# Gated linear attention and a rational MLP on one core: a sixth plain pair of feature blocks, the turned k in another bank, a new order

## The chip, the core and the metric

One core of a Trainium2 chip runs one program. TensorE (PE) multiplies matrices, VectorE (DVE), ScalarE (ACT) and GpSimd (POOL) work on elements, SyncE (SP) issues most DMAs. Each engine works through its own queue in order and waits on semaphores for the others. Time is device microseconds of an execution, the median of the runs shown.

## The reference

3072 tokens (4 batches of 768), 8 heads of 48. Per head a state decays by alpha and takes in an outer product of k and v; its product with q is the attention's output, 384 values for each token. These go through an MLP of 2048 features whose activation is a quotient of polynomials.

```
for t in range(S):
    state = alpha[:, :, t, :, None] * state + einsum('bhd,bhe->bhde', k[:, :, t], v[:, :, t])
    y[:, :, t] = einsum('bhd,bhde->bhe', q[:, :, t], state)
h = x @ w_in
P = a[0] + a[1]*h + a[2]*h*h + a[3]*h*h*h
Q = 1.0 + abs(b[0])*abs(h) + abs(b[1])*h*h
out = (P / (Q + 1e-06)) @ w_out
```

## The kernel before

**Attention** goes in 24 groups g of 128 tokens. DVE turns alpha, q and k into place (`turn_a`, `turn_qk`; the first four groups are turned by PE instead, L439, and copied by ACT, L458), scans alpha from both ends (`suffix` L476, `prefix` L488), and the results scale k and q (L497, L500). PE turns k (`k_turn`, L551), ACT copies it out (`k_evac`, L554); PE makes the scores (`sc_mm`, L518) and the values' outer products (`kv_mm`, L582). The scores are copied out in two halves, each on ACT (L539) or DVE (L541), and masked by POOL (L545); DVE adds up the state (L610, L613), and ACT or POOL places it beside the values (L568). Then PE does the attention product (`attn_mm`, L600), and ACT copies it into x (L630, L634), its rest being taken by DVE (L638).

**The MLP** is a list of jobs u. A plain job takes 256 tokens and a pair of feature blocks (2 x 128 features) through FP32 matmuls (`plain_in` L680, `plain_out` L693). A wide job takes 512 tokens and one block, with x, the weights and the result each split into a high part and a rest, and three products for one (`wide_in` L707, `wide_out` L726; the last 512 tokens use L720 and L735). The plain jobs cover the first JP = 5 pairs of the first 512 tokens, 10 jobs; wide jobs do the rest, 6 blocks of the first 512 tokens and all 16 blocks of the other five supers m of 512. Between in and out of a job stand ACT's absolute value (L762), linear term (L765) and reciprocal (L793), POOL's or ACT's parts of Q (L769, L771, L774) and five steps of DVE (L785, L789, L803, L806, L812); the last of these, called g, frees the bank of the job's input product, which is used again three jobs later (`bank(u % 3)`). Wide jobs then split the result (L815 on ACT, L819 on POOL or DVE).

**Weights** come as pairs of 32-bit words of doubles and are put together by five steps for each key (a pair of blocks of w_in, "i", or w_out, "o"): `join_scale` (L285, ACT or POOL), `join_low` (L293, DVE), `join_sign` (L297 on ACT, L299 on DVE) and `join` (L313, DVE). Keys under JP are kept whole for the plain jobs, in place; later an SP load (`bring`, L321) brings each back to be split for the wide jobs (`split_hi` L328, `split_lo`). Other keys are split at once.

**A guard** loads alpha in 18 pieces and checks its bounds, two activations of ACT for each (L865); the sums (L875, L878, L881) decide at the end whether the fast result stands.

**Banks.** ps is the accumulator memory of eight banks. Scores go to banks 4 and 5 (SCB and SCB + 1), the values' products to columns from 256 of both, the attention product to bank 4, the turned k to bank 4. A column of bank 5 (`floor_q`) holds the floor that the scans read from the fifth group on.

**The order.** Every step is declared by `add` with its engine, its steps to wait for and its engines to choose from. ORDER, a packed table of numbers, sets the sequence of all steps and which of the engines does a step that has a choice; each engine executes its steps in that order. A step waits for the steps listed with it:

```
was = [("xh", g - 1), ("xl", g - 1), ("km", g - 1), ("kv", g - 1), ("se", g - 1, 0), ("se", g - 1, 1)]
add(("kt", g), "PE", 0.38, k_turn, (g,), [("k", g)] + was + near, lat=0.13)
add(("s", g), "PE", SV[0], sc_mm, (g,), [("k", g), ("q", g), ("ke", g)] + was + near, lat=0.13)
```

Here kt is the k turn, ke its copy, s the scores, vk the values' products, se the two score copies, xh and xl the readers of the attention product, km and kv the two state sums. The builder adds waits wherever a step touches memory that another engine uses, by banks for ps.

Of the kernel before, what the change touches and what calls it, by code (L numbers as in the profile page):

```python
# [74 lines left out]


ORDER = [
    'c-jq?gO(*a5CGGi?sSs1ZQHhO+qS)XcV>35wr$(CZQHi--Zxa8Qx!=~R!X6YsiG-Sq*yr>Lm3rCMOS0hI5l3)SBunQ6;-WN',
# [4 lines left out]
    '6q=54C_Y`$DJi)sqME9rs+h`5S?H>siL<boN<cSNLaMK_tKzDvT7-*(Qc)sGO;ITt&Bi&n1k+G9%1Sw@wQ8&8;sRWTX(=6@',
    'S7+5VwG;=ahw72a9<mVU;e5<N8*x+6ZDmz@%0(HdiK?b<sr%}+%1wEwASI?GREP@Ga?D8Aba|>knW!igqwD&HUV(SiTa}lJ',
    'P;q*v+Nm}wAJwILRDznTfO@VvsVb_v3Q}FvAoW8%RXtU2wGu1QDjcXPQdKHRrRa%zrCzGL>V;Z^>v1hs4yi)xuo~s30#u(G',
    'P-$uyvH=^>8}&hzq3TqF?y1$d8Mg%0q{dW>now8OS#?wGRWH>?^;Lt_5Y?K>QX6VYZK)acQ~d)S)Hb}S+fxVXNxi5y4OQi+',
    '9c{$}*fDSpo6{}*UVT)3sUIE0?y5(iHf_f`)Q5K9SM^hUQwn~oFY2HAt^geTQemnEwWI)bBn_RYGX<;RYB+sXpVThwPk+@P',
# [50 lines left out]
    '(y#K>eGOmJFZ0WNX<y4X_bq%&-^#c4wS67m#<%q~T|3|2ckms3C*Rq3@m+m4-`)4{J$)a)!mswdd~d(juk-7Dec#vr2X6hG',
    'js',
# [1085 lines left out]
```

## Time and profile before

| | |
|---|---|
| median of 3 runs | 522.44 us (521.91 to 522.75) |
| profiled execution, its own time | 521.38 us |
| its span | 519.3 us |
| PE busy | 499.3 us, 96% |
| DVE busy | 473.2 us, 91% |
| ACT busy | 411.0 us, 79% |
| POOL busy | 404.8 us, 78% |

Busy time is that of the whole span. The terms below come from the profiled execution, which lies 1.06 us under the median.

### The profile page before, as it was taken

Reading aid. Unit: us, or ns where it says so; the run is one execution under the profiler, and the core shown is the slowest. Engines: PE = TensorE matmul, PEld = TensorE weight load, DVE = VectorE, ACT = ScalarE, POOL = GpSimd, SP = SyncE. Lnnn points to the kernel's source line nnn. Section 1 sums busy time; section 2 is a strip of 40 time slices with the busy share of each in tenths; the row PEclk is TensorE's granted clock in tenths of the full one; section 3 lists DMA queues with packets and bytes.
Section 4 is the critical chain, followed back from the end, with each engine's and each line's share of the span. In section 5 each row is a group of like instructions: output and inputs, shape, how many; then the busy total and the mean of one; then the engine's idle time right before and its main releaser. Section 6 shows DMA issues by size and latency. Waiting matters only on the chain.

```text
span 519.3 us, 13513 instructions
## 1 busy us (share of the span) xinstructions
PE 499.3 (96%) x5094; PEld 412.3 (79%) x5094; DVE 473.2 (91%) x729; ACT 411.0 (79%) x756; POOL 404.8 (78%) x419
## 2 busy tenths in 40 slices
PE   8877899999999999999999999999999999999995
PEld 7776778788887788878888788888888787789895
DVE  3997999999999999999999999999989899898793
ACT  3879999999899877868777777886878778776564
POOL 3253765989999999788989988797896779667673
PEclk9997999999999999999999999999999999999999
DMA  9989945554555545653456454344625400050001
GB/s 246 307 240 245 279 104 130 146 119 110 119 127 136 123 92 130 106 112 84 86 120 124 93 133 84 90 86 102 143 50 116 82 1 1 3 101 1 0 1 64
DMA packets 146708, 57.56 MB, mean 111 GB/s; under 512 B 133456, under 2 KB 139216, under 8 KB 146640
## 3 DMA queue, kind: packets, MB, share of 16 engines
q1 hardware_dynamic: 146496, 56.57, 46.6%
q8 instruction: 41, 0.67, 0.5%
q14 instruction: 27, 0.22, 0.1%
q10 hardware_dynamic: 144, 0.10, 0.1%
HBM read 47.98 MB, written 4.72 MB: 101 GB/s over the span
## 4 chain that ended last, share of the span: by engine, by line
PE 63%; ACT 11%; DVE 6%; POOL 6%; DMA 5%; SPq 5%; issue 4%; POOLq 0%; DVEq 0%; ACTq 0%
PE ps L707 26%; PE ps L726 22%; PE ps L600 3%; PE ps L693 3%; SPq L415 2%; PE ps L720 2%; DMA wi_words<-in_moe_w_in_dram 2%; POOL gh_gl L819 2%; ACT wo_words L297 2%; PE ps L518 2%; PE ps L582 2%; PE ps L680 2%; POOL qm L774 1%; ACT ps L793 1%; DVE t L789 1%
## 5 line engine op out<-in xcount | busy, mean ns | idle before, releaser
L707 PE MATMUL ps<-x,wi 128*128 128x512 f32 x774 | 197.7, 396 | 0.7 <-DVE t L812 0.6
L707 PEld LDWEIGHTS ps<-x,wi 128*128 128x128 f32 x774 | 142.6, 188 | 32.6 <-DVE t L812 2.6
L726 PE MATMUL ps<-gh_gl,wo 128*128 128x512 f32 x630 | 162.5, 396 | 0.1
L774 POOL TENSOR_TENSOR qm<-qm,ah 128x512 f32<-128x512 f32 x96 | 124.1, 1294 | 23.4 <-ACT qm L771 20.3
L726 PEld LDWEIGHTS ps<-gh_gl,wo 128*128 128x128 f32 x630 | 115.8, 188 | 25.6 <-POOL gh_gl L819 0.9
L819 POOL TENSOR_TENSOR gh_gl<-t,gh_gl 128x512 fp32r<-128x512 f32 x83 | 107.4, 1297 | 21.0 <-ACT gh_gl L815 12.6
L793 ACT ACTIVATE ps<-qm 128x512 f32<-128x512 f32 x96 | 57.7, 602 | 36.6 <-DVE t L789 17.7
L803 DVE SCALAR_TENSOR_TENSOR t<-t,coef,ps 128x512 f32<-128x512 f32 x96 | 70.8, 737 | 12.7 <-ACT ps L793 11.3
L765 ACT ACTIVATE t<-ps,coef 128x512 f32<-128x512 f32 x96 | 65.4, 684 | 14.2 <-POOL gh_gl L819 9.5
L789 DVE SCALAR_TENSOR_TENSOR t<-t,coef,ps 128x512 f32<-128x512 f32 x96 | 70.7, 738 | 1.5
L785 DVE TENSOR_TENSOR t<-t,ps 128x512 f32<-128x512 f32 x96 | 64.9, 677 | 6.8 <-ACT t L765 5.2
L812 DVE SCALAR_TENSOR_TENSOR t<-ps,t 128x512 f32<-128x512 f32 x96 | 65.6, 684 | 1.5
L806 DVE SCALAR_TENSOR_TENSOR ps<-qm,ps 128x512 f32<-128x512 f32 x96 | 65.8, 685 | 0.0
L762 ACT ACTIVATE ah<-ps 128x512 f32<-128x512 f32 x96 | 56.4, 590 | 9.6 <-PE ps L707 8.3
L815 ACT ACTIVATE gh_gl<-t 128x512 fp32r<-128x512 f32 x86 | 53.6, 625 | 6.6 <-DVE t L812 5.9
L769 POOL TENSOR_SCALAR qm<-ah,bab 128x512 f32<-128x512 f32 x42 | 32.4, 772 | 18.9 <-ACT ah L762 7.1
L545 POOL TENSOR_SCALAR_AFFINE_SELECT tqk<-tqk 64x512 f32<-64x512 f32 x48 | 31.4, 655 | 18.7 <-ACT tqk L539 8.2
L771 ACT ACTIVATE qm<-ah,bab 128x512 f32<-128x512 f32 x54 | 38.9, 721 | 0.5
L476 DVE TENSOR_TENSOR_SCAN tg<-ta,ps 128x528 f32<-128x528 f32 x24 | 29.7, 1241 | 8.6 <-ACT ta L458 7.3
L720 PE MATMUL ps<-wo,gh_gl 128*128 128x384 f32 x180 | 33.7, 336 | 0.0
L497 POOL TENSOR_TENSOR tqk<-tqk,tg 128x512 f32<-128x512 f32 x22 | 28.4, 1289 | 6.5 <-ACT tqk L458 6.3
L720 PEld LDWEIGHTS ps<-wo,gh_gl 128*128 128x128 f32 x180 | 31.8, 188 | 1.2
(112 smaller groups left out, 701.5 us busy)
## 6 DMA issues: line engine op xcount, KB each, us to landing
raw_a<-in_alpha_dram SPq DMA_DIRECT2D x160, 48.0 KB, 2.2
wi_words<-in_moe_w_in_dram SPq DMA_DIRECT2D x8, 768.0 KB, 6.5
wo_words<-in_moe_w_out_dram SPq DMA_DIRECT2D x8, 768.0 KB, 6.4
sv<-in_v_dram SPq DMA_DIRECT2D x48, 96.0 KB, 2.6
wr<-in_alpha_dram SPq DMA_DIRECT2D x18, 256.0 KB, 3.1
raw_qk<-in_k_dram SPq DMA_DIRECT2D x80, 48.0 KB, 2.3
raw_odd<-in_k_dram SPq DMA_DIRECT2D x80, 48.0 KB, 2.1
raw_qk<-in_q_dram SPq DMA_DIRECT2D x80, 48.0 KB, 2.3
```

Source lines behind the costliest of these rows:

```text
L707: nc.tensor.matmul(h_of(u), w(key)[:, kt * FU + f % FU, :], x[:, kt, xp, :], start=(n == 0), stop=(n == len(todo) - 1),)
L720: nc.tensor.matmul(bank(T_BANKS[tt], DM), g[:, tt * P : (tt + 1) * P], w(("o", f // FU))[:, f % FU, :], start=(f == 0 and first_w), stop=( ...
L726: nc.tensor.matmul(bank(O_BANKS[dt]), w(("o", f // FU))[:, f % FU, dt * P : (dt + 1) * P], g, start=(f == 0 and first_w), stop=(f == NF - ...
L765: nc.scalar.activation(buf(s, "t1", u), h_of(u), AF.Identity, bias=a2, scale=a3_reg)
L774: nc.gpsimd.tensor_tensor(buf(s, "qm", u), buf(s, "qm", u), buf(s, "ah", u), op=ALU.mult)
L785: nc.vector.tensor_tensor(t, t, h_of(u), op=ALU.mult)
L789: nc.vector.scalar_tensor_tensor(t, t, a1, h_of(u), op0=ALU.add, op1=ALU.mult)
L793: nc.scalar.add_instruction(mybir.InstActivation(name=nc.get_next_instruction_name(), engine=nc.scalar.engine, func=AF.Reciprocal, ins=[nc ...
L803: nc.vector.scalar_tensor_tensor(t, t, a0, h_of(u), op0=ALU.add, op1=ALU.mult)
L806: nc.vector.scalar_tensor_tensor(h_of(u), buf(s, "qm", u), Q_ONE, h_of(u), op0=ALU.add, op1=ALU.mult)
L812: nc.vector.scalar_tensor_tensor(t, h_of(u), 2.0, t, op0=ALU.subtract, op1=ALU.mult, reverse0=True)
L819: eng.tensor_tensor(buf(s, "gl", u).rearrange("p a b -> p (a b)"), buf(s, "t1", u), gh, op=ALU.subtract)
```

## The change

JP goes from 5 to 6: the first 512 tokens have 12 plain jobs and 4 wide ones, where it was 10 and 6. Jobs are 96 either way. Keys 5 of w_in and w_out are now kept whole and brought back later by two SP loads. The k turn and its copy use bank 5; the turn waits for kv and se of the group before it, no longer for xh, xl and km. The scores still wait for all six. ORDER is a new table (2733 steps where there were 2737), which also chooses engines anew: of the score copies ACT does 45 of 48 where it did 43, of the signs 13 of 16 where it did 12, of the rests of results POOL does 82 where it did 83. In a new program all lines behind the table are one less.

```diff
 ORDER = [
-    'c-jq?gO(*a5CGGi?sSs1ZQHhO+qS)XcV>35wr$(CZQHi--Zxa8Qx!=~R!X6YsiG-Sq*yr>Lm3rCMOS0hI5l3)SBunQ6;-WN',
...
+    'c-jq@gO(ji5CErpx_c1Ywr$(CZQIGs?q(6&wr$(CZQFS7AL>+{im8-BHC{ziPDNL-lvj~d6ct&KimE0kR-$64iE5!*qNb{8',
...
-JP = 5
+JP = 6
...
     def k_turn(g):
         for a in range(NPAIR):
-            nc.tensor.transpose(bank(SCB)[:, a * KW : (a + 1) * KW], tk[g % NQ][0:KW, a, :], ident[0:KW, 0:KW])
+            nc.tensor.transpose(bank(SCB + 1)[:, a * KW : (a + 1) * KW], tk[g % NQ][0:KW, a, :], ident[0:KW, 0:KW])
 
     def k_evac(g):
-        nc.scalar.activation(kts[g % NSC][:, 0 : NC4 * KW], bank(SCB, NC4 * KW), AF.Copy)
+        nc.scalar.activation(kts[g % NSC][:, 0 : NC4 * KW], bank(SCB + 1, NC4 * KW), AF.Copy)
...
-        add(("kt", g), "PE", 0.38, k_turn, (g,), [("k", g)] + was + near, lat=0.13)
+        add(("kt", g), "PE", 0.38, k_turn, (g,), [("k", g)] + was[3:] + near, lat=0.13)
```

In the rows of the order, t_100 to t_102 are the results in work of three jobs in turn, tqk_88 to tqk_90 the turned q and k of three groups in turn, ps the banks, and x3 a row that repeats. On DVE, around the score copy of group 2 (L541 before, L540 after), before:

```order
L785 TENSOR_TENSOR t_100<-t_100,ps 128x512
L488 SCALAR_TENSOR_TENSOR fp_85<-ta_84,ps 128x528
L789 SCALAR_TENSOR_TENSOR t_100<-t_100,coef,ps 128x512
L785 TENSOR_TENSOR t_101<-t_101,ps 128x512
L468 STREAM_TRANSPOSE ta_83<-raw_a_80 128x4x2x2x32
L789 SCALAR_TENSOR_TENSOR t_101<-t_101,coef,ps 128x512
L541 COPY tqk_90<-ps 64x2x4x64
L803 SCALAR_TENSOR_TENSOR t_100<-t_100,coef,ps 128x512
```

and after:

```order
L784 TENSOR_TENSOR t_100<-t_100,ps 128x512
L612 TENSOR_TENSOR st_95<-st_94,ps 112x192
L788 SCALAR_TENSOR_TENSOR t_100<-t_100,coef,ps 128x512
L540 COPY tqk_90<-ps 64x8x64
L292 TENSOR_SCALAR wo_words<-wo_words 128x768
L312 SCALAR_TENSOR_TENSOR wi_words<-wr_77,wi_words 128x6x128
L784 TENSOR_TENSOR t_101<-t_101,ps 128x512
L802 SCALAR_TENSOR_TENSOR t_100<-t_100,coef,ps 128x512
```

The scan (L488) and the turn of alpha (L468) have gone from ahead of the copy, which is now the other half of the scores (64x8x64), and the state sum of group 2 (L612) stands ahead of it. On PE, from the attention of group 3 (the L600 row of 32 with tqk_88) and the output of job 2 (L693 with t_102) to the k turn of group 4 (L551), before; the L680 row of six between the two rows of t_102 is the input of job 5:

```order
L680 MATMUL ps<-x_whole,wi_words 128x256 x3
L600 MATMUL ps<-tqk_88,sv_92 32x64 x32
L693 MATMUL ps<-t_102,wo_words 128x256 x3
L680 MATMUL ps<-x_whole,wi_words 128x256 x6
L693 MATMUL ps<-t_102,wo_words 128x256 x3
L551 MATMUL ps<-ident,tqk_89 128x112 x4
```

and after, where the input of job 5 is the L679 row of six:

```order
L692 MATMUL ps<-t_101,wo_words 128x256 x6
L679 MATMUL ps<-x_whole,wi_words 128x256 x6
L599 MATMUL ps<-tqk_88,sv_92 32x64 x32
L692 MATMUL ps<-t_102,wo_words 128x256 x3
L550 MATMUL ps<-ident,tqk_89 128x112 x4
L692 MATMUL ps<-t_102,wo_words 128x256 x3
```

The input of job 5 has moved ahead of the attention of group 3 and of the first half of job 2's output, and the k turn of group 4 stands two rows behind that attention where it stood four behind.

## Rows read from the trace of the kernel before

**Rows 1.** The page: busy time by engine, and granted clock in 40 slices

```profile
PE 499.3 (96%) x5094; PEld 412.3 (79%) x5094; DVE 473.2 (91%) x729; ACT 411.0 (79%) x756; POOL 404.8 (78%) x419
...
PEclk9997999999999999999999999999999999999999
```

**Rows 2.** Groups of PE, 62 to 511 us: busy, mean ns, idle ahead, releasers

```profile
L707 PE MATMUL ps<-x,wi 128*128 128x512 f32 x774 | 197.7, 396 | 0.7 <-DVE t L812 0.6
...
L680 PE MATMUL ps<-x_whole,wi_words 128*128 128x256 f32 x60 | 14.3, 385 | 1.2 <-DVE t L812 1.0 <-ACT x_whole L630 0.2
L518 PE MATMUL ps<-tqk 48*64 48x64 f32 x640 | 13.8, 223 | 0.0
```

**Rows 3.** Stretches: us, busy of PE, PEld, DVE, ACT, POOL, clock, DMA share, GB/s

```profile
8.80:61.10 52.30, 42.00 (x724) 36.63 (x721) 48.30 (x76) 43.99 (x73) 22.56 (x29) 0.93 0.97 269
...
62.00:511.00 449.00, 446.67 (x4312) 365.71 (x4312) 421.76 (x648) 361.82 (x673) 377.63 (x364) 1.00 0.41 90
```

**Rows 4.** PE in order of time: start, us, line, idle ahead and its releaser

```profile
6.10 2.06 PE L439 MATMUL ps<-ident,raw_a 128*128 128x128 f32 x16
...
35.63 1.60 PE L680 MATMUL ps<-x_whole,wi_words 128*128 128x128 f32 x12
40.66 1.11 PE L582 MATMUL ps<-sv,kt 64*64 64x48 f32 x32 [3.42 <-ACT tqk L539]
...
45.35 3.83 PE L680 MATMUL ps<-x_whole,wi_words 128*128 128x256 f32 x12
...
59.62 1.10 PE L600 MATMUL ps<-tqk,sv 128*32 128x64 f32 x64
61.08 1.56 PE L693 MATMUL ps<-t,wo_words 128*128 128x256 f32 x6 [0.35 <-DVE t L812]
62.88 1.35 PE L680 MATMUL ps<-x_whole,wi_words 128*128 128x256 f32 x5 [0.24 <-ACT x_whole L630]
```

**Rows 5.** ACT in order of time

```profile
40.01 0.59 ACT L539 ACTIVATE tqk<-ps 64x512 f32<-64x512 f32 x1 [3.00 <-DVE tqk L541]
...
42.32 1.93 ACT L297 ACTIVATE wo_words<-wo_words 128x768 f16<-128x768 f32 x1
```

**Rows 6.** DVE in order of time

```profile
33.34 1.03 DVE L299 TENSOR_SCALAR wo_words<-wo_words 128x768 uint16<-128x768 uint16 x1
...
35.27 1.24 DVE L488 TENSOR_TENSOR_SCAN fp<-ta,ps 128x528 f32<-128x528 f32 x1
...
38.93 0.67 DVE L541 COPY tqk<-ps 64x512 f32<-64x512 f32 x1
41.26 0.75 DVE L803 SCALAR_TENSOR_TENSOR t<-t,coef,ps 128x512 f32<-128x512 f32 x1 [1.67 <-ACT ps L793]
41.93 0.55 DVE L293 TENSOR_SCALAR wi_words<-wi_words 128x768 uint32<-128x768 uint32 x1
...
60.93 1.25 DVE L488 TENSOR_TENSOR_SCAN fp<-ta,ps 128x528 f32<-128x528 f32 x1
```

**Rows 7.** Chain that ended last: start, us, what

```profile
67.42 2.60 PE ps L680 x12
...
108.75 2.59 PE ps L693 x12
...
122.58 2.04 PE ps L707 x9
...
255.49 2.04 PE ps L726 x9
```

**Rows 8.** The tile raw_a in the first 9 us: its load's issue, and time to landing

```profile
L422 SPq DMA_DIRECT2D raw_a<-in_alpha_dram x1: 573/573/573, 1.4 to 1.4; - x1
...
DMA to landing us min/median/max: 4.5/4.5/4.5
```

**Rows 9.** Chain that ended last, 505 us to the end

```profile
513.90 0.41 ACT wr L865
...
514.41 0.90 ACT wr L865 x3
...
515.33 0.20 DVE tot_beyond L875
```

More of the change, by code (lines that the diff above doesn't have):

```diff
@@ L83 @@
[L83 to L87, printed above, removed]
@@ L138 @@
[L138 to L139 removed]
+    'c-jq@gO(ji5CErpx_c1Ywr$(CZQIGs?q(6&wr$(CZQFS7AL>+{im8-BHC{ziPDNL-lvj~d6ct&KimE0kR-$64iE5!*qNb{8',
+    'YPy=FCaWoGrCP0)s&#6STCUcp#cHiurd9+t2G*+{*b{qUY!z3<Q8Uyk)f;cBfjB5=gX)9*aRBzkemEGzFg$3pnyF@~t!k%=',
+    'r{<~DYEvMs8iMEb1${AiC=NqVXVrYQO9e1pAikQdwy5D4fg^(sD6N8Un;L<k7>pq}SItp})ee<gol*PM5w%<G4dhh^RT`CE',
+    'jl!eqn98Gw7O3rNkD7|3@seg5gE6VJI<3yB>nfirt1j!YD0C%w9F_|lQpW?99PLx%aXQWjGURC{MxqHg5hvl~pu{Sv%CBNk',
@@ new lines @@
+    '9Ewb_DQ-wSice7}i7KO#sRWdeqS94$N!3<$RUK7col=+81$9DA!D+Yz6Hzp}r4mze)mpVtk5pw<Rkc+Y)iw24C8rdWin3BY',
+    'm6B%TEWE0#1?sCLl$J89tSTL~Q`hu$9i6h#(xB{=n$pk}bza?2F=!6vpxjiLPO5ph3|C-#l}%+)*;P(TPZ`LnT$G1ytBmwo',
+    'JyC^KQ8gEf(0p8u3vdzMRSR)3W}=7cfqJg)sJxVq-m1o`sd}Z}sHdu!Dx!+3Dyq85Pe~~m6{TWSk}6UqT8TIGO<kNa(<&@L',
+    'S*Re@r$SVjnyDtL3YDUJ>Xz=Tx~li;nR=mKs&}dcm8LROoyt-Tsv5ExtI?LAPpTXRsnxg!0q(1{xD~f!1L~rhs}HK1>aNz|',
+    'M%;uoX+3VhkE#~+RzFo=^;d1fhSWHu2{ocVsx7sn_S8?+rlwSf%F|BVg*&hUb)aU{oH|l}H9!qgLzIHS>W6AUw{?gbs#;QK',
@@ new lines @@
+    'I)tB9C+bagsSov~fq_<3k0R6`^+o+t-&GgtO8w}Y(r`zQPz>E@Aa$q1LH$F5D40S>U=R(U!4yh8XqXD9Fd7~hLcbNlFBKQQ',
+    'DuQSb6%wd85E)ui8`_O~aRlwbBRG@};6dDn`|&7R2&Z8b1tKUuBvgq4kst=dgP7pKKtkwAy=Xj5pkQ?j@9KMcB8^ldX%bDQ',
+    'Q7Tl8qNy~RrqNuQNAoF69mf+mh5|I47SLjHa0*Z2MVvy@X$B>Nv2+^G;Tc>)GwCwUqSz1}Qm70nqe=;}AOWO?RIo7Q0vZ(_',
+    'IE#zuJg%lSw3gP>21*P`VH~ZajkJ_5;WA38?&1BQO|+acLRv@xSzt45p%t`;_R>B&KwD`x&7u8th_2v${XlP{!;}QB;x#--',
+    'sRE<b7<HD;(RMmdnF2@XB3+{EcoUOD8psUE;08XxN0<$c(lNS&cX1`Hq6>5jZ{tHu51AkX+@t&SkjAQ=lpWGRR=7-8=r~=a',
@@ new lines @@
+    'YxEc&>PLD9J))d2E^vY#(-V4&C+RvprCoG`ZqjbLMNjYneWUO6gDg9KM$hRN<$zr9lk!6W$PEQl5%3&|3qvs|4*4K26oeP_',
+    'k|OgTdPT44FBMc#xg<p6-}H~3;{SMX6pqd@I3^>XqSJJSZd0Ma8%n@;=o!AiJn$S};w#LdYCs{#sd5Dpaw5J<Z|NN+;iUW?',
+    '6LTz%%^&bR#o^cZzos}NXW~MfnX_^>euLGa1Qdl*@QJ=qGX6lxIR!Hd7iPn8IUZMmicl3QsLGIqE2>I?(ohakaw<;E*|{=T',
+    ';rLvHi*gAr#%VYmr{(mVfs1nqRZ`{PoLnkU3F^T|%*DC6B<JBK+?1<wHLlJzxD3?fT3i-NabC{H@9+<P!fH?(+Cwd<3k_65',
+    ')hN)6Yjblh&1JX+x8yopmOo=%ZpHPuHJ9TrSf2l4eQv|~xd0dB2Hce^a7FIM!#KbVpe?uKR?q=jLOZAckM$E>iOa)R{Dw7D',
@@ new lines @@
+    'P1T)yaxZQH&7m{Yg!bHndvik=&Osc^<9Px%<VM_>J8-Q)C+^IBcm)5$4yvOH;f`Df>O)`d$KP=x|H4oX<NiFEL3aua;03&p',
+    'f8#(N#EoGJ|G=L(iIooL2wu#KcnL4%E<BhU!APFUqj)24;%VF!+CW?A3$39)G=)CULUn>>5P<32QlWmTwI;ocm-7l9!b7=L',
+    'U<}XTnfy$z<ZiH;xAH8W&7zwCYoq(Y0O$xq;Uf)%;m`$E@o3({+j%UH<3oIy=kjX4%vZRF>J7u77mR_yFcJpA4z}9sH5^$-',
+    '(cK}cj;`nMJf6=-_!w{Fo!nC$<*OVFyLdM{y_T<WwBSfOhJLPlKuo=dk8@Ax71+!BIF?SNL*N9T<QMuBpXM`sop174e!@@r',
+    '8Nc8g99zfLqhK_QfH*pde$KCWD%|3+Fa&~N9k1sNyq~}F0Y1pz_#B_-3w)6i=%o5K$J2NCHQ(iXoLIl)pZtdZ@LNu(<LhL4',
@@ new lines @@
+    'GK`0Cm<J1B0)#?x9R~OL0bk;W{8GQtQRN5!;uQKfzvI9BkKc1NNhZnV1ApY`5<_B2N|_EyKvGC5i6yZm0v19_om!8BxiBAA',
+    '!9<87sdPq-@`xYvC(bT8<THO^Ei5D=M&e2ay#~@qJjtx%O9Ck&X(gTR<(EPlomz5AI!UY3>rBB}^mm>Dlc2Ak2D9KZ<<nVp',
+    'dYJ(kB%_p+no>)0hkE%+ktLVpm27$~<dJ-mNixe;SOHe%z)DCci6pTkk))DEvdT=D4f&;j6qG{JN?J=PDHEDs_w!|?w3L%N',
+    '@><uH!tzFE*Ew{3DK8bIfz%DHCk>^IRFq1RO^Qk}DI&$Ctu&I#(p&mSJISf5NHwW01$4pS_EJb!l^U`ew!>!F3Cmy$EQY<X',
+    '4LV3i=_LE1u{4np5-NFgU&*U;>D;=hG?V7iPx|}bzO3#aIzSe|a##YJptE$5FbS7~&{eugcPXbM<TRXwjc^Kf!5&x*>tUdb',
@@ new lines @@
+    'l0h<9rph!~2P0*)43VL72!_c9m@YFzXUP~DD>G!aw2+q4LkjD+x{rUS$H^QiqI*g&DXIf9T*k{>nJ3F+xvY>?p{r$rtdwH9',
+    'xV{8C-~#M}%WxKs!3ij#%j*ik^JR^c)C**-ER=OJz@LNdvO|I-SVClyOq9toMNY^fDWwm<akvPNV7**{`>;VO>Wy+3cF9gT',
+    'DW|2h-Xy2wjO>+tat(He9)UfwUvA1`xg}+ECH-EXhr93u&dGT>AO~f$)X{h3tQ>{P`nFWjcSG;V5?Lx+WUGA8RdqFeUk=GD',
+    'xgZy1o4l68azv`@8oHLQtslrG8R#F%9XJD5;iw#wdb)wWEWhQEJeK;wHT4y_DmUScJckEx4_?Ax{}f)p4|oXg<h{I=y1}jW',
+    'b@(I4<(fQ^DCVg=lMnJ5KFTL~2DjlWJci%!7ox~FxB-7fg?*NPg64~8^9G`t=q84VZ3g)-@EL~rPtZ_*)ITATG}71QhCG)S',
@@ new lines @@
+    '@=}KSukuN!F=@>$cnfh1n3!R)%n;v3f0OS*hK-oUI<ARl(wPil8BKa)j5W?=GMP;l^Fx~ICOWUlXX2aurhsXt3z|YEfk|lE',
+    '>Ywro3Y)Cv9h5WCOnLK5yoqEYo5UuGX|J=Hf6!95(#>@RQ^XWC*-d?u$gJ=!bPki#R0^wXhWm=9oo-+nn)gu56gQ1c69ZVn',
+    'lr&XLRg=`DFsY1_WTug+W~!T}ri1CAKkF~LndzuI>5e9s$!%(wnx>a7Wj?@1=%PF8fRBWKAjpUKPNumD_P@Ym3)9l%F<neo',
+    'Q_IvgolRHWO%K=Ibt}`_3^b)p88gTXHc|0AAPx;1W_kyAGu@5CKDvkLY08>9rmh)f>Y34IhzXb;x{Vp(`|2>?%k(z0O<Oa^',
+    'v@`9EV7QNl7NcNK-A_k&!ZBuCn8x8I$OM}ZGv4&qeM~>o*Nio>FeawL7?=X1qeFuu%mg#h#Kxo;7uT5nW~~`u=9*9+YUYP6',
@@ new lines @@
+    'FpQJTWb;*z^z+O@GeA!<>&%9*FtgEo(*yNjy~s>8i_Lm7NC)W<9d7oTeI~+;G|4bB4$(vP60^xHHF0pWS!RamfSzV%m|#6Z',
+    '?>7lBR8KcsOgubjmYW0SkQt{}n5|};*=`P-Bj%_%XJ(r7=AzkQW|^JlzIk9)npI}CiH`{}Odm7H%?WeTJTxE76_W;&U}8*(',
+    'qkMAAfSK@uxfFKUj1RtQcA4Ggqxr5Mn@8rF`JtbhXXd)OVKU<<bIN=+U(8K&%RDj9%^vgB+%`opHD<>|m=+6QK1_!ZI$VD<',
+    '6ZFL3@8*ShX<nI;dX)ZQM*G)hj2^4=V-75cIWZ5W$BdX2C+X3;Fy_M3=8QRO-k7{N#!v8QwPl+Ht^H|!ncs%2*jV<CiEZQ9',
+    'xYpUb=AL<LChIA>5EjEqm>W}?YFHLin=)7xlbf-=6&ma9ACtgFvXO0So5sE~?@czGtK)_LGs;f#KlLvi#TLaDSRN~46)cBo',
@@ new lines @@
+    'ZDCu)rn7$y*z`7&ovNeS=r)E;XfuSzw~6dDJzZzEiER>_(PptpZ55l<7PZlAOk33!v&C%*J3}Y4$!#`U($3eVY<4?am$qeW',
+    'S)0Qy2+nDn+Ge&mF4Wa*b(_LAw>82`VNKh@&eZdQXX!P1j!tP)*_Pq0Y&ly3YuVbijxC9~Y&V<R*0uF)ecQlxw>@kx+uF9V',
+    'd2C*r-xjoOZ9Ci02JCRVNH5mqZLkfp6>TNk-gdARupQRI3bv>1V=LQ6c7mN~8{3YyiS2B=*uFN@_O|_Oe;Z~8*nxJTU1Wdj',
+    'aellnjUnM9?AqXP8(}-yu6B@}WT%8rwS#RP9AbysC3><QY3t%2y;Lu@OYJB-%}%#V>~gzI&#*J?3cF4(*Ax9RyV8!fW9%$D',
+    '+pf^7f>+tqc8%R+H`^_Cj@@Rr+8uV79c#zg@wNum#3tAjt7Bzsj+1>`Y=rsjG(XpFxAW{_d&JJS3+!sWK6s_xs5j`^SRXg(',
@@ new lines @@
+    'EB30L;-~uQz8TK+ZLlRa#KySR&hR_!E_>7-4_{|b*xh!IJ!VhZzk09TXZPDvwjTb|*X&dK%&xZ^>_&Ut-m<stY=7FGv72=R',
+    '+@fFDt$L2{hTX9>p0yqDoIPL<+C%oay%B!X-m!P>YkSXrv%B@4;Pdu^eQ96Wi}t&1kN2&0m+WP`P0#W>gLmnUxL3ci4{R5F',
+    'Xn)!t_Lu!_-`YRcIqxF5NA|IOV&B=n_PzaJ6S#zKyWXKAyH3~{_XQu&|EzNR^+Em7ezxGyC32s_wM*g@C3aC9xvm)1MRU>J',
+    'A)V1>a+zHg_r-qwf3QyJ(;Dcoj^SduST1WsQkUH&bIIKioy{H9$MkW1M(1#`T?&`drE;lVAy?RmGcK-+=T7L8`m8>ubGlqE',
+    'w@c&VxMD88OXrY^y5bQfTpp*XmMiH>xx6l)D_{%RxxTb3<I1{nuC`0>inuy1t*h%=yEd+^Yv(e!{H~9i=gYf#5%paI*U&X`',
@@ new lines @@
+    '9bG5a*fnwOBRaUwu8XVS`nrB@K*T^d-!JrCT~k-U6?FYwH#f))b`@PESJ{QSFgMLjcg@@aAMUET8m@{P;##<tuDOeFt=!0n',
+    'QLek|;fA_lF5s5C;ckYT717hJaHHKAH`9%E<J@@H%k_4_Zl#;;g4`-M$4zi^-CDQK&2#hJM7O{#bgSJOx85ysJKRne;zqd1',
+    'ZkIdhPPs{Lw_EJaxG8R`TjG|w({4}1Ubn$*bY~+rxy^2$+wTszWp1lG=eD?m?z}tX4!a}ng1hK0xy$Z~yX9`XyY7y==U%%v',
+    '?ycMAwz~)Jp*!l{xsUF?d*nX3$L@)H>fT3ua97=D_r?8jf89TK&4E|`nfvOrCy$=}F?ZaZa8Z3Uf89m*&s_{3)5r4P+;?}w',
+    '-E=?P3-{6`^U3}HvG=ik9B+MGAJ3=oDSfJuseOE(z^C!ATte@>_t||8pVQ|anbxQC>3s(O)BSS4T_T^ym+&QhMqktC@_Bte',
@@ L140 @@
+    'U)q=R`F#Oj(3kRMd|4mKNA|URCSS*w_l0~tU%^-OQG8~f*eCHxeO+JJ*Y^#4L*K~P_E~&ZpUoHb#e5}S*;nyJd~sjRSNBzY',
+    '4Zp}Q_Dg(Y-^4fd&3yBbHQiEQ-L>#7eO1@WxAtxPa=*;C_3eCn-@$kEoqT8C#dq~Rd{5uaclRs(D!<zQ2MYC>EC',
 ]
```

54 lines of the change are left out of this document (removed).

## The prediction

> **What bounds the kernel now.** I read the page first: TensorE (PE) is busy for 96% of the span [rows 1]. So I asked where PE waits. In the groups of PE's instructions from 62 us to 511 us the idle time ahead of all of them comes to about 2 us, 1.2 of it ahead of the plain input matmuls and 0.7 ahead of the wide ones, and none ahead of the scores [rows 2]; the same stretch in the windows view has PE busy for 446.67 of 449 us [rows 3]. The time is therefore three parts: a start in which PE waits for its operands, the PE work itself, and a short tail. An edit pays only if it shortens the start, removes PE work or shortens the tail; work taken from the other engines behind 62 us is free already.
>
> The start is where time is lost. PE's order of time shows it [rows 4]: after the input half at 35.63 us come 3.42 us without work until the values of group 2 (L582), which the view puts on ACT's score copy, and the input matmuls of job 5 start at 62.88. The releases lead back to DVE [rows 5, 6]: ACT's score copy (L539) at 40.01 sat idle 3.00 us for DVE's copy of the other half, which DVE reached only at 38.93, since the scan at 35.27 and four other steps stood ahead of it in its queue. From 8.80 to 61.10 us DVE has 48.30 us of work in 52.30 [rows 3]: DVE's queue sets the start, with 4.0 us of holes. The clock fell too: the fourth slice of forty, 39 to 52 us, was granted 7 tenths, where nearly all others have 9 [rows 1].
>
> **Part 1, PE work (a cost).** The change turns two wide jobs into two plain ones. A plain job is 24 records, a wide one 9 in and 9 out. The chain gives plain records back to back as 2.60 us for 12, and 2.59 on the output side, wide ones as 2.04 for 9, on both sides [rows 7]. A plain job is 2.60 + 2.59 = 5.19, a wide one 2.04 + 2.04 = 4.08; two jobs cost 2 x 1.11 = **+2.2 us**. Nothing hides it, since PE is full there [rows 2]. The high and low halves of the results that the two wide jobs no longer need, two on ACT and two on POOL, lay beside a full PE and count nothing. Two loads that bring a joined weight back, 393 KB each, join SP's queue; they are wanted by wide jobs of the second 512 tokens, and from 62 us on the DMA engines are busy at a share of 0.41 [rows 3], so zero, and about one DMA's landing (4.5 us [rows 8]) if a wide job had to wait for one.
>
> **Part 2, the start (the gain).** Of the new order I counted what stands ahead of the last step of job 2 on DVE (its g, which frees the bank that job 5 fills). It ends at 61.02 (the next DVE step starts at 60.93, overlapping by the pipeline [rows 6]). Gone from ahead of it are three score copies, two signs, a turned k, a low word and a join; new ahead are a turned k, a score copy, a sign and a join. Net: two score copies at 0.67 and one sign at 1.03, with a low word at 0.55 [rows 6]; 2 x 0.67 + 1.03 + 0.55 = 2.9, of which I take 2.6, as steps overlap by about 0.1. The score copy of group 2 that DVE did so late is now ACT's, and ACT's other copy is DVE's, and no scan stands right ahead of it there: so the waits for ACT's reciprocal behind it (1.67 at 41.26 the longest [rows 6]) and four smaller ones, 3.3 of the 4.0 us of holes, should go. Then g of job 2 ends at 61.02 - 2.6 - 3.3 = 55.1 and the input of job 5 starts some 0.6 later, 55.7 in place of 62.88: 7.2 us earlier. Not all of that is gain: attention of group 3 (1.10 at 59.62) and half the output of job 2 (at 61.08; 1.3 at full clock, by half of 2.59 [rows 4, 7]) now stand behind that input and not ahead of it, 2.3 us after overlap. That is 4.9. From below: were only the list shorter and the holes to stay, 61.02 - 2.6 = 58.4, job 5 at 59.0, 3.9 - 2.3 = 1.6. From above: all holes gone, 4.9 + 0.7 = 5.6. A walk through the new queues leaves PE two gaps of about 3 and 2.5 us, so the clock may fall again: the 12 records at 45.35 took 3.83 us [rows 4] where 12 take 2.60 [rows 7], 1.2 more. I take **-4.0**, near the upper end and less part of a clock loss. Behind this DVE runs only just ahead of PE until about 110 us, which is why I do not go higher.
>
> The first load is alpha where it was k. It landed 4.5 us after its issue at 1.4 [rows 8], so by 5.9, and PE's first turn, of alpha, starts at 6.10, its 16 matmuls back to back with what PE did before, as the view puts no idle on it [rows 4]: nothing to win, and nothing lost, since k is turned 2 us later.
>
> **Part 3, the k turn in the second bank.** The turn waits no longer for both readers of the last group's attention, but for three steps that wrote or read the scores and values. It can stand next to attention, or ahead of it, where it stood several places behind. PE is full there, so an earlier turn earns nothing by itself; what it may cost is a new wait. The scans of DVE take their floor from a column of that second bank. Score and value matmuls wrote into that bank before, behind the same scans, and no idle time stands ahead of the scores [rows 2]. I take zero. From below it could give back at most the 2 us of idle that PE has at all; above, the rival has it.
> The Trainium skill has a rule that speaks against this edit (PSUM — Partial Sum Buffer, "PSUM bank collisions raise a hardware error"): two engines may not touch one bank in the same partitions at once even at different addresses, so accesses must be guarded by bank. By it a turn must wait out every scan that reads the floor, which the old bank did not ask of it; by the row the same waits cost the scores nothing. By the rule the time would be that of rival (b), by the row that of the forecast; on what stands ahead of the scores the trace does not bear the rule's price out.
>
> **Part 4, the tail.** The end of the chain has two of the input guards of ACT (L865) behind the last copy out: 0.41 at 513.90 and 0.90 at 514.41 for what the trace gives as three pieces, and then the verdict's sum at 515.33 [rows 9]. In the new table all guards stand ahead of the last copies. ACT has room (79% busy [rows 1]), so 0.5 to 1.0 goes; **-0.7**.
>
> **Sum.** -4.0 + 2.2 - 0.7 = -2.5 on the profiled execution of 521.38 (span 519.3 and 2.1 around it): 518.9. The median of the runs lies 1.06 above that execution, so 519.9 as a median.
>
> **Rivals.** (a) ACT takes DVE's place, slower. ACT's list up to the reciprocal of job 2 grows by 1.8 us, with more signs at 1.93 on it [rows 5]; ACT worked without a long hole in 40 to 62 us. If the score copies still come late for each other, the 3.00 us hole [rows 5] moves to ACT's queue with the 1.8: of the lead of 4.9 then 4.9 - 3.3 - 1.8 = -0.2 is left, and the change is +0.2 + 2.2 - 0.7 = +1.7, or 524.1. It decides as soon as the lead is under 1.5, where part 1 less part 4 eats all of it. For it: DVE and ACT hand tiles to and fro in every job. Against: ACT's long steps there are joins of weights, which the new table spreads.
> (b) The k turn waits for scans, slower. In about 11 of the 24 groups a scan stands just ahead; one takes 1.24 us [rows 6], so half a scan on average is 0.6 and 11 of them 6.8 us: 526.7; a third of that leaves nothing of the gain. Against it speaks the idle of 0.0 ahead of the scores [rows 2].
> (c) The gains are real but near their low ends: -1.6 + 2.2 - 0.5 = +0.1, with a part of the holes gone -0.8: no change, about 522.
>
> **Chances.** A measurement can tell about 0.2%, 1 us, from no change. The forecast has 0.66 for faster by more than that (under 521.4), (c) 0.13 for within it, (a) 0.14 and (b) 0.07 for slower. The range is to leave out 2 in 10: upward it takes in (c) and the near part of (a), 523.3; downward the sum of the lower ends, -5.6 + 2.2 - 1.0 = -4.4 or 518.0, and 1.2 more, somewhat over half of the 2 us of idle of part 3: 516.8.
>
> **What would show it.** Right: the L539 row of ACT for group 2 without an idle of 3 us, job 5's input near 55.7 us, PE 2.2 us busier past 62 us, no guard behind the last copy. Wrong: idle ahead of L550 (the k turn's new line) put on DVE's scans, which is (b); DVE idle in 40 to 60 us put on ACT's reciprocals, which is (a); or PE idle behind 62 us, which would say that the lead was given back later.

## The result, and the profile after

The changed kernel takes 514.52 us (513.59 to 515.09) where the kernel before, on the same chip, takes 522.60: a ratio of 0.985, interval 0.983 to 0.987, or 8.1 us less. The forecast was faster by 2.5, range 516.8 to 523.3: the right side, but the gain is three times what was forecast and lies outside the range. The profiled execution took 514.17 (span 512.4, where before has 519.3), so 6.9 us of span are to be found. Of the other 1.2 us, 0.9 come from the choice of executions (that of before lies 1.2 us under its median here, that of the changed kernel 0.35 under), and 0.3 lie outside the spans.

PE's order of time holds marks that both kernels pass. First after, then before: the input of job 7, ahead of which PE executes the very same steps in both; the input of job 16, with which the second 512 tokens begin; the input of job 80.

```profile
71.06 1.13 PE L679 MATMUL ps<-x_whole,wi_words 128*128 128x256 f32 x4
...
125.69 1.17 PE L706 MATMUL ps<-x,wi 128*128 128x512 f32 x4
...
435.07 1.29 PE L706 MATMUL ps<-x,wi 128*128 128x512 f32 x5
```

```profile
75.05 1.13 PE L680 MATMUL ps<-x_whole,wi_words 128*128 128x256 f32 x4 [1.00 <-DVE t L812]
...
128.43 0.84 PE L707 MATMUL ps<-x,wi 128*128 128x512 f32 x3
...
441.11 1.07 PE L707 MATMUL ps<-x,wi 128*128 128x512 f32 x4
```

| stretch | before | after | difference | for the same PE work | forecast |
|---|---|---|---|---|---|
| start, to job 7's input | 75.05 | 71.06 | -4.0 | -4.0 | -4.0 |
| job 7 to job 16, where the plain jobs are | 53.38 | 54.63 | +1.3 | +1.5 | +2.2 |
| job 16 to job 80 | 312.68 | 309.38 | -3.3 | -2.9 | 0 |
| job 80 to the end of the span | 78.2 | 77.3 | -0.9 | -1.5 | -0.7 |

The fifth column counts the trace's matmuls. In the changed kernel one k turn (0.4 us) falls just ahead of job 16's input and not behind it, and three wide matmuls (0.7 us) fall behind job 80's input that came ahead of job 16's; the column sets them back. The surprise is the third row. PE is as full there as before; the groups of PE (columns as in [rows 2], 62 to 505 us) show that the idle time has gone from 2 us to some 0.5, which is not enough:

```profile
L706 PE MATMUL ps<-x,wi 128*128 128x512 f32 x756 | 189.3, 393 | 0.3 <-DVE t L811 0.3
...
L679 PE MATMUL ps<-x_whole,wi_words 128*128 128x256 f32 x72 | 17.2, 384 | 0.1
L517 PE MATMUL ps<-tqk 48*64 48x64 f32 x640 | 13.9, 223 | 0.0
...
L550 PE MATMUL ps<-ident,tqk 112*128 112x112 f32 x80 | 11.9, 271 | 0.1
```

The mean of a wide matmul fell from 396 to 393 ns [rows 2]: 3 ns on some 1400 of them, 4 us, which the view counts as busy. What is in it shows when the trace is read from start to start of PE's matmuls. The usual distance of two wide ones is 227 ns. PE leaves them for attention's small ones (a run of small matmuls) and comes back. In the kernel before, PE's order of time from 200 us on has attention (L600) alone, the k turn (L551) alone, and values and scores (L582, L518) together:

```profile
200.13 1.29 PE L707 MATMUL ps<-x,wi 128*128 128x512 f32 x5
201.35 1.10 PE L600 MATMUL ps<-tqk,sv 128*32 128x64 f32 x64
202.38 3.69 PE L726 MATMUL ps<-gh_gl,wo 128*128 128x512 f32 x15
...
209.78 0.55 PE L551 MATMUL ps<-ident,tqk 112*128 112x112 f32 x4
210.09 0.94 PE L726 MATMUL ps<-gh_gl,wo 128*128 128x512 f32 x3
```

and after, the turn (L550) right behind attention (L599):

```profile
199.51 1.52 PE L725 MATMUL ps<-gh_gl,wo 128*128 128x512 f32 x6
200.96 1.10 PE L599 MATMUL ps<-tqk,sv 128*32 128x64 f32 x64
201.99 0.60 PE L550 MATMUL ps<-ident,tqk 112*128 112x112 f32 x4
202.36 1.62 PE L725 MATMUL ps<-gh_gl,wo 128*128 128x512 f32 x6
```

Around attention the start-to-start distances are 318 ns going in and 337 ns from the first to the second wide matmul behind it, for 227; behind the k turn the latter is 313; and the seven or eight wide matmuls that follow a run are up to 10 ns longer each, some 0.03 us in all. All distances between the two marks, job 16 and job 80, add up like this (a run is what it adds to the wide matmuls around it; "following" are the small excesses of wide matmuls, up to 33 ns each, "waits" the larger ones not beside a run):

| us, (count) | before | after |
|---|---|---|
| wide matmuls at 227 ns | 262.2 (1155) | 262.2 (1155) |
| attention, k turn, apart or as one run | 26.6 (16 + 16) | 25.1 (15 as one, 1 attention alone) |
| scores and values | 21.0 (16) | 21.1 (16) |
| following | 1.35 | 0.51 |
| waits | 1.5 | 0.5 |
| sum | 312.7 | 309.4 |

Of the 3.3 us, 0.4 are the k turn that falls ahead of the mark, 1.0 lie in the runs, 0.8 in what follows them and 1.0 in waits for operands. Over the whole program PE's order has 73 runs before and 52 after.

The tail, in the chain that ended last, has no guard left between the last copy and the verdict's sum (compare [rows 9]):

```profile
507.52 0.34 ACT parts L752
507.86 0.02 issue
507.88 0.36 DVE parts L754
508.24 0.11 DVE tot_beyond L874
```

### The profile page after: what moved, and what is told of

It reads as the page before. It is cut to its first block, busy times and chain, and to the rows that moved or that the text cites. A ratio compares the mean times of both kernels' runs of the same rounds, so it can differ in the third digit from the quotient of the medians.

```text
span 512.4 us, 13531 instructions
## 1 busy us (share of the span) xinstructions
PE 497.8 (97%) x5106; PEld 415.4 (81%) x5106; DVE 469.7 (92%) x725; ACT 413.9 (81%) x750; POOL 404.2 (79%) x425
## 4 chain that ended last, share of the span: by engine, by line
PE 61%; POOL 9%; DMA 7%; ACT 7%; DVE 6%; SPq 4%; issue 3%; POOLq 0%; DVEq 0%; ACTq 0%
PE ps L706 26%; PE ps L725 19%; PE ps L719 6%; PE ps L599 3%; DMA wi_words<-in_moe_w_in_dram 3%; POOL qm L773 3%; DMA wo_words<-in_moe_w_out_dram 2%; SPq L414 2%; PE ps L692 2%; POOL gh_gl L818 2%; PE ps L517 2%; PE ps L550 1%; DVE t L802 1%; PE ps L581 1%; DVE ps L805 1%
## 5 line engine op out<-in xcount | busy, mean ns | idle before, releaser
L706 PE MATMUL ps<-x,wi 128*128 128x512 f32 x756 | 189.3, 393 | 0.3 <-DVE t L811 0.3
L706 PEld LDWEIGHTS ps<-x,wi 128*128 128x128 f32 x756 | 140.5, 188 | 29.4 <-DVE t L811 0.8
L725 PE MATMUL ps<-gh_gl,wo 128*128 128x512 f32 x612 | 154.6, 393 | 0.0
L725 PEld LDWEIGHTS ps<-gh_gl,wo 128*128 128x128 f32 x612 | 113.3, 188 | 23.9 <-ACT ah L761 0.4
L818 POOL TENSOR_TENSOR gh_gl<-t,gh_gl 128x512 fp32r<-128x512 f32 x82 | 105.9, 1295 | 12.6 <-ACT gh_gl L814 11.0
L814 ACT ACTIVATE gh_gl<-t 128x512 fp32r<-128x512 f32 x84 | 52.5, 628 | 14.1 <-DVE t L811 11.5
L679 PE MATMUL ps<-x_whole,wi_words 128*128 128x256 f32 (+1 forms) x180 | 36.9, 356 | 4.3 <-DVE wi_words L312 2.7
L475 DVE TENSOR_TENSOR_SCAN tg<-ta,ps 128x528 f32<-128x528 f32 x24 | 29.9, 1245 | 8.2 <-ACT ta L457 7.7
L679 PEld LDWEIGHTS ps<-x_whole,wi_words 128*128 128x128 f32 x180 | 29.9, 203 | 8.6 <-DVE wi_words L312 2.8
```

Of the source, the lines that this page charges most:

```text
L679: nc.tensor.matmul(h_of(u)[:, ff * SEG + c0 : ff * SEG + c1], whole(("i", j))[:, kt * FU + ff, :], x_whole[:, kt, m * SEG + c0 : m * SEG + ...
L706: nc.tensor.matmul(h_of(u), w(key)[:, kt * FU + f % FU, :], x[:, kt, xp, :], start=(n == 0), stop=(n == len(todo) - 1),)
L725: nc.tensor.matmul(bank(O_BANKS[dt]), w(("o", f // FU))[:, f % FU, dt * P : (dt + 1) * P], g, start=(f == 0 and first_w), stop=(f == NF - ...
L818: eng.tensor_tensor(buf(s, "gl", u).rearrange("p a b -> p (a b)"), buf(s, "t1", u), gh, op=ALU.subtract)
```

## The experiments

Times are medians; where several kernels ran together they share the runs of the kernel before. Diffs of the order name the steps that were moved, since ORDER itself is packed. Single runs of the changed kernel spread more (513.4 to 517.0) than those of the kernel before (521.2 to 522.7 in the longest series), so differences under 1 us between its variants are not read from times alone.

**The changed kernel again.** 

> The changed kernel once more, so that the next three are compared with it on one chip. All theories: 514.5 us, some 8 us under the kernel before.

 It took 515.33, ratio 0.988 (0.986 to 0.990). 

> The changed kernel a third time, as the measure for the next two on the same chip: 514 to 515.5.

 It took 514.95, ratio 0.987 (0.985 to 0.989). All 15 runs together have a median of 514.9. The stretch from job 16 to job 80 measures 309.4, 309.4 and 309.3 in the three traces.

**The k turn apart from attention.**

```diff
 attn_mm(g-1)
-k_turn(g)
 next wide step
+k_turn(g)
```

> The changed kernel, its k turn still in bank 5, but from group 9 on the next wide step of PE (3 to 5 matmuls, about 0.7 to 1.1 us) stands between the attention of one group and the k turn of the next, in 15 groups. Theory of runs: each time PE leaves the wide matmuls for attention's small ones and comes back costs about 0.15 us, whatever the small ones are; with 15 runs more PE needs 15 x 0.15 = 2.3 us more, 516.8. Rival of feeding: the turn's early place helps because scores come earlier; 0.7 us later is then worth at most some tenths, under 514.9. Rival of the table: where the turn stands is worth nothing and the steady gain comes from other steps of the new order; 514.5.

 It took 517.84, ratio 0.994 (0.991 to 0.996), 2.5 over the changed kernel beside it. The stretch from job 16 to job 80 is 312.3, 2.9 longer with the same matmuls in it, and what the kernel before has but for its one turn more (312.7 less 0.4). The runs of attention and turn take 1.3 more and what follows them 0.55, as the theory of runs has it; 0.7 more lies in the runs of scores and values and 0.4 in waits, which is feeding. So the place is worth the steady gain of 2.9, by both theories: 1.8 by runs and 1.1 by feeding, more than the tenths that its theory gave it. The theory of the table falls.

**Scores and values apart.**

```diff
 sc_mm(g)
-kv_mm(g)
 next wide step
+kv_mm(g)
```

> The changed kernel with its k turn beside attention as it is, but from group 9 on the next wide step of PE stands between the scores and the values' products, which stood side by side, in 15 groups. Theory of runs: the same price as for the k turn, 15 x 0.15 = 2.3 us, 516.8, since only the number of runs counts. Rivals of feeding and of the table: 514.5 to 514.9.

 It took 522.1, ratio 1.001 (1.000 to 1.002), 6.8 over the changed kernel, three times what was expected, and the whole gain of the change is gone. PE's order of time:

```profile
209.27 0.84 PE L706 MATMUL ps<-x,wi 128*128 128x512 f32 x3
210.04 0.69 PE L517 MATMUL ps<-tqk 48*64 48x64 f32 x32
210.67 0.97 PE L725 MATMUL ps<-gh_gl,wo 128*128 128x512 f32 x3
211.56 0.68 PE L581 MATMUL ps<-sv,kt 64*64 64x48 f32 x32
212.18 0.50 PE L725 MATMUL ps<-gh_gl,wo 128*128 128x512 f32 x1
```

Scores alone add 0.83 us (median of 15) and values alone 0.82, where the two as one run add 1.28: 0.37 for one run more, in the mean 0.42 with the few that waited; 15 of them are 6.3 of the 7.4 us by which the stretch grew. So runs are what costs, but not all cost the same. A k turn alone adds 0.41 where it adds 0.35 behind attention, 0.06 by medians, and about 0.05 less in what follows. The turn is the one kind of small matmul here that fills nearly the whole array (112*128 in its rows, like the wide ones' 128*128); scores, values and attention use parts of it (48*64, 64*64, 128*32), and it is going over to those and back that costs. The distances from start to start show it (medians from job 16 to job 80, in the kernels before, changed and with the turn apart): from a wide matmul to attention, scores or values 318 to 326 ns, to a turn alone 237; from the last matmul of attention, scores or values 149 ns to a wide one and 150 to the turn, from the turn to a wide one 27; from scores to values, side by side, 39. The 337 ns behind a run are not part of it, since the turn, too, has 313 there. The Trainium skill states it (TensorEngine Tiling (Array Packing), "Tiling Modes", Key Properties): a change of the tiling mode drains the engine. The trace agrees in where the longer distances stand, and gives them a size; that a drain is what they are is not shown by it.

**The bank alone.** The kernel before, its own table and places, and:

```diff
-            nc.tensor.transpose(bank(SCB)[:, a * KW : (a + 1) * KW], tk[g % NQ][0:KW, a, :], ident[0:KW, 0:KW])
+            nc.tensor.transpose(bank(SCB + 1)[:, a * KW : (a + 1) * KW], tk[g % NQ][0:KW, a, :], ident[0:KW, 0:KW])
...
-        nc.scalar.activation(kts[g % NSC][:, 0 : NC4 * KW], bank(SCB, NC4 * KW), AF.Copy)
+        nc.scalar.activation(kts[g % NSC][:, 0 : NC4 * KW], bank(SCB + 1, NC4 * KW), AF.Copy)
...
-        add(("kt", g), "PE", 0.38, k_turn, (g,), [("k", g)] + was + near, lat=0.13)
+        add(("kt", g), "PE", 0.38, k_turn, (g,), [("k", g)] + was[3:] + near, lat=0.13)
```

> The kernel before with its own table and five plain pairs; only the k turn and its copy use bank 5 and the turn waits for three steps less. Theory of runs: the turn stands where it stood, as many runs as before, so no change: 522.5. Rival of the scans (the prediction's b): turns wait for scans that read the floor in bank 5, up to 6.8 us more. Rival of the bank: the fewer waits alone let the turn go earlier, 1 to 3 us less.

 It took 537.33, ratio 1.031 (1.029 to 1.032): 15.7 us slower. No theory had this size, but rival (b) of the prediction had its place. Behind 62 us the idle ahead of PE's groups comes to 13.8 us where it was 2 [rows 2]. Waits there that have to do with turns and scans (who waited for whom, us in total, times, longest):

```profile
DVE tg L476 <- PE ps L551: 5.1, 2, 4.0
...
ACT kt L554 <- PE ps L551: 4.3, 5, 1.1
DVE tg L476 <- ACT kt L554: 4.2, 4, 2.1
POOL tqk L500 <- DVE fp L488: 3.8, 2, 3.6
...
DVE fp L488 <- PE ps L551: 3.0, 1, 3.0
...
PE ps L551 <- DVE fp L488: 2.8, 2, 1.6
```

Only the last line is the wait that the prediction priced, a turn behind a scan. ACT's wait for the turn was there before the edit:

```profile
ACT kt L554 <- PE ps L551: 3.5, 4, 1.1
```

The three lines of DVE, 12.3 us together, go the other way: a scan stands in DVE's queue behind a turn or its copy, and all of DVE's work behind it stands too. One place at 67 us in DVE's order of time, and PE's behind it:

```profile
62.77 0.71 DVE L803 SCALAR_TENSOR_TENSOR t<-t,coef,ps 128x512 f32<-128x512 f32 x1
67.51 1.25 DVE L476 TENSOR_TENSOR_SCAN tg<-ta,ps 128x528 f32<-128x528 f32 x1 [4.04 <-PE ps L551]
```

```profile
66.92 0.55 PE L551 MATMUL ps<-ident,tqk 112*128 112x112 f32 x4
70.66 4.47 PE L680 MATMUL ps<-x_whole,wi_words 128*128 128x256 f32 x12 [3.19 <-DVE t L812]
```

DVE stands 4.04 us for the turn, which PE reaches only at 66.92, behind plain matmuls; then PE stands 3.19 for DVE. The bank by itself, in the old table, is a loss; in the changed kernel turns and scans stand so that hardly one waits (no line of this kind over 0.6 us is left in the changed kernel but ACT's copy, once 3.1 for the turn).

**The floor out of the bank.**

```diff
-        return floor_p if g < G3 else floor_q
+        return floor_p if g < G3 else floor_s
```

> The kernel before with the k turn in bank 5 as in the run on the bank alone (537.3 us), but from group 4 on the scans read their floor from a tile outside the banks, so that turns and scans share no bank. Theory of the shared bank: the loss came from scans of DVE waiting for the turn and its copy, and turns for scans, in queues not laid out for it; without the shared bank it goes, 521 to 523. Rival of the place: bank 5 is late for the turn for another reason (scores and values of the group before); the loss stays, 535 or more.

 It took 565.52, slower again. The scans, with their floor outside the banks, sit idle for nothing now, but each takes longer, 2246 and 1929 ns in the mean where it took 1247 and 1245:

```profile
L476 DVE TENSOR_TENSOR_SCAN tg<-ta,floor_s 128x528 f32<-128x528 f32 x20 | 44.9, 2246 | 0.0
L488 DVE TENSOR_TENSOR_SCAN fp<-ta,floor_s 128x528 f32<-128x528 f32 x20 | 38.6, 1929 | 0.0
```

The waits of scans for turns are gone, as the theory of the shared bank says, but the time says nothing on it, since some 34 us of DVE work (20 x 1.0 and 20 x 0.7) came with the edit. So that the 15.7 us are these waits is read from the trace of the run before, and not shown by a run of its own.

**Back to the old bank under the new table.** From group 9 on, with xh and xl set right behind attention:

```diff
-bank(SCB + 1)
+bank(SCB + (g < 9))
...
-[("k", g)] + was[3:] + near
+[("k", g)] + was[3 * (g < 9) :] + near
```

> The changed kernel with the k turn back in bank 4 from group 9 on, as far as the waits allow: the two readers of the last attention stand right behind it on ACT and DVE, and the turn three wide steps behind it on PE, the scores two more behind that. Theory of runs: it costs what the turn apart in bank 5 cost, 2 to 3 us over the changed kernel, 517 to 518; the bank is worth nothing beyond letting the turn stand beside attention. Rival of the bank: bank 5 also spares waits; 4 us or more over the changed kernel, 519 and up.

 It took 567.82. This does not decide what it was to decide. The readers that I set early block their engines' queues: behind 130 us DVE's L644 waits 26.4 us in 13 places for ACT's L629, and that one 23.2 for attention. What the old bank costs in a table made for it stays open; the kernel before is the only such table here.

**A score copy in the start.** The kernel before, the copy (2, 0) of group 2 by ACT:

```diff
-DVE: sc_evac(2, 0), behind a scan and four more steps
+ACT: sc_evac(2, 0), next to sc_evac(2, 1)
```

> The kernel before with one score copy of group 2 done by ACT, next to the other, where DVE did it behind a scan and four more steps. Theory of the prediction's part 2: the 3.00 us hole of ACT and most of the 3.42 us hole of PE go, DVE's list is 0.67 shorter, and job 7's input starts 2.5 to 4 us earlier than 75.05; 519 to 520. Rival (a): ACT's list becomes the bound and eats it; within 1 us of 522.

 It took 519.66, ratio 0.996 (0.994 to 0.997): 1.9 us faster. The trace is of the longest of its five executions, 522.61, so it shows where the holes went and not what that is worth. PE and ACT, in order of time:

```profile
37.88 0.68 PE L581 MATMUL ps<-sv,kt 64*64 64x48 f32 x32 [0.93 <-ACT tqk L538]
41.48 1.94 PE L599 MATMUL ps<-tqk,sv 128*32 128x64 f32 x64 [2.92 <-DVE st L609]
```

```profile
36.64 1.19 ACT L538 ACTIVATE tqk<-ps 64x512 f32<-64x512 f32 x2
```

ACT's hole of 3.00 is gone and PE's of 3.42 is 0.93 [rows 4, 5]; a part comes back as 2.92 us, for 1.72 before, ahead of attention. Job 7's input starts at 73.95 there, 1.1 us earlier than before and not 2.5 to 4. By the medians, one edit of one step is about half of the start's gain. (The lines are one less in this kernel too.)

**The guards alone.** The kernel before, the last two guards ahead of the last copies:

```diff
+guard(16, 1), guard(17, 1)
 last_done(...)
-guard(16, 1), guard(17, 1)
```

> The kernel before with the last two guard activations of ACT ahead of the last copies out, behind the last split of a result, where ACT has a hole of 2.5 us. Theory of the prediction's part 4: the verdict comes 1.0 to 1.1 us earlier, 521.0 to 521.5. Rival: the output's stores or SP's queue set the end, and nothing changes.

 It took 520.84, ratio 0.9983 (0.9974 to 0.9993): 0.7 us less, 0.4 to 1.4 by the interval, where the theory had 1.0 to 1.1; part 4, at 0.7, holds. Its start, the same code as before, puts job 7's input at 76.47 where the other trace has 75.05; so a start of the kernel before is read to about 1.4 us.

**PE work doubled in one place.** The changed kernel with

```diff
-        for kt in range(KT):
+        for kt in list(range(KT)) * (2 if u in (10, 11) else 1):
```

in `plain_in`. 

> The changed kernel with the input matmuls of plain jobs 10 and 11 (near 100 us) made twice over, 24 records more on PE and no work more on any other engine. Theory of the prediction's part 1, that PE work behind the start is paid in full: 24 x 0.216 = 5.2 us more, 519.7 to 520.5 where the changed kernel has 514.5 to 515.3. Rival: PE still waits for DVE so near the start, and a part of it hides there: under 518.

 It took 518.94, which lies between the two theories: 0.8 under the range of the first, and 4.1 over the 514.9 of all runs of the changed kernel. The traces decide: the stretch from job 7 to job 16 is 59.7 us where the third trace of the changed kernel has 54.7, 5.0 longer, and the spans are 517.0 and 511.8, 5.2 apart. The row of one doubled pair is 5.45 us for 24 records where it was 2.86 for 12. Part 1's price holds, and next to nothing hides it at 100 us.

**Two tries at a still faster kernel.** Group 2's scaled q and group 3's scaled k by POOL:

```diff
-DVE: mult_q(2), mult_k(3)
+POOL: mult_q(2), mult_k(3)
```

> The changed kernel with the scaled q of group 2 and the scaled k of group 3 made by POOL, which stands idle there, and not by DVE, whose queue sets the start. If DVE's list sets the start, 0.69 + 0.73 less and a hole of 0.48 gone make the start 1 to 1.9 us shorter: 512.6 to 513.6 where the changed kernel has 514.5. Rival: POOL's 1.28 us for each makes the scores of group 2 or the turn of group 3 late, and it is the same or up to 1 us worse.

 It took 515.85, ratio 0.989 (0.987 to 0.991): no gain. What DVE's list lost comes back as waits: 0.75 us for the values at 32.34 and 0.71 for POOL's mask at 35.69, and the join that job 2's input waits for still starts at 36.16, where the changed kernel has 36.01. So DVE's list alone does not set the start there; the rival holds. Three small edits for PE:

```diff
 attn_mm(5)
+k_turn(6)
 next wide steps
-k_turn(6)
...
+sc_mm(g)
 kv_mm(g)
-sc_mm(g)
...
+wide_in(20, 1)
 wide_out(16, hi, "gh")
```

> The changed kernel with small edits of its order for PE: the k turn of group 6 beside attention too, scores ahead of the values' products in three more groups (1.28 us for a run in that order by the trace, 1.36 in the other), and the second input half of job 20 ahead of job 16's output, which waited 0.15 to 0.36 us there. Theory of runs: 0.1 + 3 x 0.08 + 0.2 = 0.5 to 0.7 us under the changed kernel. Rival: other waits take their place, within 0.3 us of it.

 It took 516.65, ratio 0.990 (0.989 to 0.992), 1.7 over the changed kernel beside it, worse than either theory had it. The steady stretch is the same, 309.4; the turn of group 6, set beside attention, waits for a scan:

```profile
95.91 1.10 PE L599 MATMUL ps<-tqk,sv 128*32 128x64 f32 x64
98.62 0.57 PE L550 MATMUL ps<-ident,tqk 112*128 112x112 f32 x4 [1.60 <-DVE tg L475]
```

That is rival (b) in one place, 1.60 us of it; in the changed kernel, with 12 plain matmuls between attention and this turn, the turn does not wait. None of the runs beats the changed kernel.

## Why the prediction was wrong

**What bounds the kernel**: right as to the parts, start, PE work, tail. Wrong in what it took from it, that behind 62 us an edit can only win PE's idle or its counted records. PE's busy time holds 0.1 us (a turn) to 0.4 us (scores and values) for each run more of small matmuls between wide ones.

**Part 1**, +2.2: right in its price, since the doubled inputs cost 5.0 to 5.2 us where 5.2 were due. From job 7 to job 16 it shows as +1.5 for the same PE work, with 9 runs for 10 in the stretch; where the other 0.7 went is not shown, and the sixth pair by itself was not run.

**Part 2**, -4.0: the way is right, and -4.0 is what job 7 shows, but that it fits to a tenth is luck. Job 5's input starts at 57.40, not 55.7, 5.5 us earlier and not 7.2. DVE's work ahead of it is 45.72 us for 48.30 [rows 3], the 2.6 of the list; of its holes of 4.0 us 2.9 are left, where the prediction let 3.3 of them go. Against that, 1.5 us of the lead are given back by job 7 and not 2.3, since the idle of 1.00 ahead of job 7 went too, and the clock's part, for which 0.9 had been set aside, is within the 5.5 already. With the other trace of the same start, 76.47, the gain would be 5.4. ACT's score copy has next to no hole, as the working says (0.38 us for 3.00 [rows 5]). The stretch up to job 5's input (columns as in [rows 3]) and the copy:

```profile
8.80:57.40 48.60, 40.79 (x660) 35.48 (x658) 45.72 (x72) 44.99 (x74) 20.10 (x30) 0.96 0.95 251
```

```profile
34.19 0.59 ACT L538 ACTIVATE tqk<-ps 64x512 f32<-64x512 f32 x1 [0.38 <-DVE st L612]
```

PE's two gaps, forecast as 3 and 2.5 us, came as 2.66 and 0.66, and the 24 records between them took 4.57 us, where 24 like them took 2.94 at 30.29 in the kernel before: the granted clock was 0.50, the lower of its two levels, from 38 to 40 us. Over 39 to 52 us it was 0.92, where the kernel before has 0.74.

```profile
37.02 4.57 PE L679 MATMUL ps<-x_whole,wi_words 128*128 128x128 f32 x24 [2.66 <-DVE wi_words L312]
42.25 1.56 PE L679 MATMUL ps<-x_whole,wi_words 128*128 128x256 f32 x6 [0.66 <-DVE t L811]
```

**Part 3**, "I take zero": this is the step that failed. The prediction saw that the turn now stands next to attention and said that an earlier turn earns nothing where PE is full; and it set the most that it could give back to the 2 us of idle. It priced the turn's time and not its neighbours. Beside attention a turn saves one run: 1.8 us from job 16 to job 80 by runs and what follows them, and 1.0 in waits, which is within the 2 us of idle. Moving the turn away again cost 2.9. A row that would have warned stood in the chain of the kernel before: nine wide matmuls take 2.26 us right behind attention, where the prediction took 2.04 for nine.

```profile
189.58 1.03 PE ps L600 x64
190.61 2.26 PE ps L726 x9
...
199.38 2.04 PE ps L707 x9
```

On the rule of the Trainium skill on banks (PSUM — Partial Sum Buffer, "PSUM bank collisions raise a hardware error"): the prediction let the idle of 0.0 ahead of the scores speak against it. The rule was at work all the same. The trace of before could not show it for the turn, whose bank the scans did not share; in the run on the bank alone the edit cost 15.7 us, by the waits for the most part in the direction that the prediction did not consider, scans behind turns. The changed kernel, with the same bank and another table, shows next to none of these waits.

**Part 4**, -0.7: right by the guards alone, 0.7; in the traces the verdict comes 1.1 us sooner behind PE's last products. PE also waits about 0.7 us less behind job 80, which the prediction did not have, and 0.2 is lost behind the verdict.

**The rivals**: (a) did not come. (b) did not come in the changed kernel, but is real (above). From the sum of -2.5 to the 6.9 of span it is 2.9 from job 16 to job 80, 0.8 in the tail and 0.7 that part 1 came out under its price. Part 3 is by far the largest of the three.
